# First stage of a long-convolution kernel: v pieces in output tiles, ten x buffers, one load for w1 and window, zeros multiplied at the start

## The chip, the cores and the metric

The kernel runs on one core of one Trainium2 chip. The metric is device microseconds of one execution, as the median of several; lower is better. In the views below PE is the matmul engine (TensorE) and PEld its weight loads, DVE is VectorE, ACT is ScalarE, POOL is GpSimd, and SP is SyncE, which does nothing here but issue DMAs. All engines run their own instructions strictly in program order and wait for each other by semaphores.

## What is computed

A causal convolution of length 12480 over 128 channels, done with FFTs, and then two feed-forward layers on the result:

```python
h_mlp = np.maximum(pos_emb @ w1, 0.0) @ w2          # filter, S x 128, hidden size 64
h_filt = h_mlp * np.exp(-0.01 * np.arange(S))[:, None]
u = x * v
Uf = np.fft.rfft(u, n=2 * S, axis=1)
Hf = np.fft.rfft(h_filt, n=2 * S, axis=0)
y = np.fft.irfft(Uf * Hf[None], n=2 * S, axis=1)[:, :S]
a = (x * y).reshape(S, 128)
h = np.maximum(a @ moe_w_in, 0.0);  a = (h * h) @ moe_w_out       # hidden size 2048
h = a @ moe2_w_in;  out = np.where(h > 0, h, np.exp(np.minimum(h, 0)) - 1) @ moe2_w_out
```

All inputs are float32, apart from the four feed-forward weights, which the kernel gets as 64-bit words and decodes.

## The kernel before

The FFT of length 181 x 127 is cut in two factors. `phase1` (the first stage, about the first 110 us of the span) does the factor of 181 by matmuls with a table `t1`, first for the filter and then for u. `phase2` does the factor of 127, multiplies the spectra and writes the product to DRAM; `phase3`, about four fifths of the span, does the inverse factor of 181 and the two feed-forward layers. The change touches `phase1` alone.

Inside `phase1` the work runs in four parts, and the code is written in the order in which each engine gets it:

- Eight filter steps (`zstep(s)`, "z steps" below): PE multiplies the piece `post[:, s]` of the position table (partly loaded by `load_pos`) by `w1`, which lies twice on the diagonal of a 128 x 128 block of zeros; 8 matmuls of 128 columns, 16 passes in the trace, L237. DVE takes the result out of PSUM with relu and the window (2 instructions, L241) into a buffer `fb`; then POOL adds and DVE subtracts its two halves (L246) into `fold`, which lies in `xu[2]` (the trace's m).
- Sixteen filter transform steps: `s1(i, ...)` with columns of `fold`, 8 matmuls of 182 columns, 16 passes, L263; ACT takes each result out into `xr` (L132 is the helper `copy`).
- The input pieces: x and v come in sixteen pairs. `load_xv(j)` issues four DMAs on SP (x piece and v piece, each as 98 rows and 1 row, 396 KB together). `ufold(j)` is three DVE instructions: v = x * v (L254), sum of its halves into x (L255), difference into x (L129). Before, x pieces have seven buffers (NX, tag xc) and v pieces three (NV, tag vc). Pieces 0 to 6 are loaded and folded beside the filter steps; after them piece j + 7 is loaded and folded behind the two transform steps that read piece j.
- Thirty-two u transform steps ("x steps"): `s1(i, ...)` on piece i // 2, again 16 passes of L263. Each result is taken out in four copies into the output tiles `xu[0]`, `xu[1]`, `xu[2]` (m in the trace) and `xt`. For i below 18 all four are ACT's (L132); from i = 18 on the first two are DVE's (L270) and ACT does the other two.

PSUM holds four result tiles for all of these steps (three rotate in pool `pss`; every fourth step uses `ps4`, which is closed near the end, at the 46th result, for a tile of the next stage). `prologue(i)` puts the first instructions of phase 2 between the x steps: loads of w2, g and six tables tb at i = 15, matmuls on the filter at i = 24 and i = 29.

So three queues matter around the change: SP, where the load of a piece waits for the buffer that it overwrites (x: for PE's reading of the piece seven before, v: for DVE's fold of the piece three before) and everything behind it waits too; DVE, where the copies of x steps 18 to 31 stand behind the last fold; and PE, which can run at most as many steps ahead as PSUM has tiles.

Of the kernel before, what the change touches and what calls it, by code (L numbers as in the profile page):

```python
# [10 lines left out]

F32 = mybir.dt.float32
F32R = mybir.dt.float32r
# [2 lines left out]
ALU = mybir.AluOpType  # L16
# [4 lines left out]
S = 12480  # L21
D = 128
E = 64
# [6 lines left out]
K1 = N1 // 2 + 1  # L30
NP = (K1 + 1) // 2
R = 99
# [9 lines left out]
WDEC = 11  # L42
OFF = 3
LAG1 = 2
NX = 7
NV = 3
NS1 = 46


def _angle(num, den):  # L50
# [18 lines left out]
def tables():  # L69
    n1 = np.arange(R)  # L70
    k1 = np.arange(K1)
    k2 = np.arange(N2)
    pe, po = np.arange(CEN + 1), np.arange(1, CEN + 1)
    t = {}
    th = _angle(n1[:, None] * k1[None, :], N1)
    t["t1"] = np.stack([np.cos(th), -np.sin(th), -np.cos(th)], axis=2).reshape(R, 3 * K1)
    tf = np.zeros((2 * NP, N2, N2))
    k = k1[:, None, None] + N1 * k2[None, None, :]
    tf[:K1, :CEN + 1] = np.cos(_angle(pe[None, :, None] * k, L))
    tf[:K1, 0] = 0.5  # L80
    tf[:K1, CEN + 1:] = np.sin(_angle(po[None, :, None] * k, L))
    t["tf"] = np.zeros((NP, 128, 2 * N2))
    t["tf"][:, :N2] = tf.reshape(NP, 2, N2, N2).swapaxes(1, 2).reshape(NP, N2, 2 * N2)
    th = _angle(k2[:, None] * pe[None, :], N2)
    g = np.zeros((128, 128))
    g[:N2, 0] = 1.0
    g[:N2, 1:N2:2] = np.cos(th)[:, 1:]
    g[:N2, 2:N2:2] = np.sin(th)[:, 1:]
    t["g"] = g
    order = [s * p for right, left, _ in _tiles() for s, ps in ((1, right), (-1, left)) for p in ps]  # L90
    c = np.where(k1 == 0, 1.0, 2.0)[:, None, None] / L
    th = _angle(k1[:, None, None] * (np.array(order)[None, :, None] + N2 * n1[None, None, :]), L)
    t["t3"] = np.stack([c * np.cos(th), -c * np.sin(th)], axis=2).reshape(K1, N2 * 2 * R)
    th = _angle((k[2 * PD:, 0, :, None, None] *
                 (np.array(order)[:SIZES[0], None] + N2 * n1[None, :R - 1])[None, None]), L).reshape(KD, N2, -1)
    t["t4"] = np.zeros((128, 2 * th[:, 0].size))
    t["t4"][:N2] = (2.0 / L * np.stack([np.cos(th), -np.sin(th)], axis=1)).transpose(2, 0, 1, 3).reshape(N2, -1)
    pos = _taps().astype(np.float32)
    ok = (pos >= 0) & (pos < S)
    win = np.where(ok, np.exp(np.float32(-0.01) * np.where(ok, pos, np.float32(0.0))), 0.0)  # L100
    t["win"] = win.transpose(2, 0, 1).reshape(R, 8, 2, 4, 2).transpose(0, 1, 2, 4, 3).reshape(R, 128)
    return {k: np.ascontiguousarray(a, dtype=np.float32) for k, a in t.items()}


# [14 lines left out]
class Build:  # L119
# [14 lines left out]
    def setup(self):  # L134
        nc = self.nc
        const = self.const = self.pool("const")
        self.dram = self.pool("dram", 1, DRAM)
        self.ident = const.tile([128, 128], F32, name="ident")
        make_identity(nc, self.ident)
        self.zero = const.tile([128, 2], F32, name="zero")  # L140
        nc.vector.memset(self.zero, 0.0)
        self.ebias = const.tile([128, 2], F32, name="ebias")
        nc.vector.memset(self.ebias[:, 0:1], 1151.0)
        nc.vector.memset(self.ebias[:, 1:2], 255.0 * 8388608.0)
        self.t1 = const.tile([R, K1, 3], F32, name="t1")
        self.Z = self.dram.tile([K1, 128, 2 * D], F32, name="Zd")
        self.wp = self.pool("wp")
        self.tiles = _tiles()
        self.st = {}
# [28 lines left out]
    def phase1(self):  # L178
        nc, a = self.nc, self.a
        with ExitStack() as ctx1:  # L180
# [7 lines left out]
            def stile(a, b):  # L188
                ns[0] += 1
                if ns[0] % 4 == 0 and ns[0] < NS1:  # L190
                    return ps4.tile([128, a, b], F32, tag="s", name="s")
                if ns[0] == NS1:
                    ctxs.close()
                    self.psb.append(self.ctx.enter_context(
                        self.tc.tile_pool(name="psb0", bufs=1, space=PSUM, side="right")))
                return pss.tile([128, a, b], F32, tag="s", name="s")
# [3 lines left out]
            self.xt = self.mid.tile([128, KTAIL * 2 * D], F32, name="xt")  # L200
            self.p2 = self.pool("p2")
            xvp = self.right.enter_context(self.tc.tile_pool(name="xv", bufs=1, side="right"))
            fbp = self.right.enter_context(self.tc.tile_pool(name="fb", bufs=2, side="right"))
            win, w1 = self.xt[:R, :128].rearrange("p (s c h n) -> p s c h n", s=8, c=2, h=2), self.xt[:, 128:256]
            post = self.xr[:, :64 * R].rearrange("p (s w) -> p s w", s=8)
            fold = self.xu[2][:R, :2 * C1 * E].rearrange("p (o n e) -> p o n e", o=2, e=E)

# [4 lines left out]

            def load_xv(j):
                for i, (d, nm, n) in enumerate(((xs, "xc", NX), (vs, "vc", NV))):
                    t = d[j] = xvp.tile([R, 8, 2, C1], F32, tag=nm, name=nm, bufs=n)
                    t = t.rearrange("p d h n -> p (d h n)")
                    for b, e in ((0, R - 1), (R - 1, R)):
                        nc.sync.dma_start(out=t[b:e], in_=a["xv"][j, i, b:e])

            nc.vector.memset(w1, 0.0)  # L220
            load_pos(0, 1)
            for p in range(2):
                nc.sync.dma_start(out=w1[E * p:E * p + E, E * p:E * p + E], in_=a["w1"])
            nc.sync.dma_start(out=self.xt[:R, :128], in_=a["win"])
            for b, e in ((1, 2), (2, 4), (4, 8)):
                load_pos(b, e)
            nc.sync.dma_start(out=self.t1.rearrange("p k a -> p (k a)"), in_=a["t1"])
            for j in range(NV):
                load_xv(j)

            def zstep(s):
                ps = stile(2, 512)
                z = ps[:R].rearrange("p c (h n e) -> p c h n e", h=2, e=E)
                for c in range(2):
                    for q in range(4):
                        i = 4 * c + q
                        nc.tensor.matmul(ps[:R, c, 128 * q:128 * q + 128], lhsT=post[:, s, i * R:i * R + R], rhs=w1,  # L237
                                         start=(q == 0), stop=(q == 3))
                f = fbp.tile([R, 2, 2, 4, E], F32, tag="f", name="fb")
                for c in range(2):  # L240
                    nc.vector.scalar_tensor_tensor(  # L241
                        out=f[:, c], in0=z[:, c], scalar=0.0,
                        in1=win[:, s, c].unsqueeze(3).to_broadcast([R, 2, 4, E]), op0=ALU.max, op1=ALU.mult)
                f = f.rearrange("p c h n e -> p c h (n e)")
                for o, (eng, op) in enumerate(((nc.gpsimd, ALU.add), (nc.vector, ALU.subtract))):
                    eng.tensor_tensor(out=fold[:, o, 8 * s:8 * s + 8].rearrange("p (c n) e -> p c (n e)", c=2),  # L246
                                      in0=f[:, :, 0], in1=f[:, :, 1], op=op)

            for s in range(8):
                zstep(s)  # L250
# [7 lines left out]
            def s1(i, fb, dst, w):  # L258
                ps = stile(2, 512)
                pv = ps[:, :, :4 * K1].rearrange("p b (c e) -> p b c e", e=2)  # L260
                for j in range(4):
                    for q, (b, e) in enumerate(((0, C1), (C1, N2))):
                        nc.tensor.matmul(pv[b:e, j // 2, :, j % 2], lhsT=fb[j][q], rhs=self.t1[:, :, q:q + 2],  # L263
                                         start=(j % 2 == 0), stop=(j % 2 == 1))
                b = 0
                for o, n in dst:
                    o = o.rearrange("p (c d) -> p c d", d=w)[:N2, :, 4 * i:4 * i + 4]
                    o, z = o.rearrange("p c (b e) -> p c b e", e=2), pv[:N2, :, b:b + n].rearrange("p b c e -> p c b e")
                    if n == 32 and i >= 2 * (16 - NX):
                        nc.vector.tensor_copy(o, z)  # L270
                    else:
                        self.copy(o, z)
                    b += n

            for j in range(NX):
                ufold(j)
                if j + NV < NX:
                    load_xv(j + NV)
                for i in range(2 * j, 2 * j + 2):
                    s1(i, [(fold[:, 0, :, 4 * i + c], fold[:, 1, 1:, 4 * i + c]) for c in range(4)],  # L280
                       [(self.xr, 2 * K1)], E)
            for i in range(2 * NX, E // 4):
                s1(i, [(fold[:, 0, :, 4 * i + c], fold[:, 1, 1:, 4 * i + c]) for c in range(4)], [(self.xr, 2 * K1)], E)
            dst = [(t, n) for t, n in zip(self.xu + [self.xt], (32, 32, 64, 2 * KTAIL))]
            self.raw = {}
# [557 lines left out]
```

## Time and profile before

| | us |
|---|---|
| median of 3 runs | 1429.74 |
| lowest and highest run | 1426.77, 1432.49 |
| the profiled execution | 1427.98 |
| its span, first to last instruction | 1426.2 |

| engine | busy us | share of the span |
|---|---|---|
| PE | 1372.2 | 96% |
| DVE | 1199.8 | 84% |
| ACT | 1109.0 | 78% |
| POOL | 617.6 | 43% |

The shares are averages over all three phases, and phase 3 with its matmuls rules them. A change of the first stage is read from windows and timelines of the first 110 us alone. The profiled execution lies 1.76 us under the median, inside the spread of the runs.

### The profile page before, as it was taken

Reading aid. Unit: us, or ns where it says so; the run is one execution under the profiler, and the core shown is the slowest. Engines: PE = TensorE matmul, PEld = TensorE weight load, DVE = VectorE, ACT = ScalarE, POOL = GpSimd, SP = SyncE. Lnnn points to the kernel's source line nnn. Section 1 sums busy time; section 2 is a strip of 40 time slices with the busy share of each in tenths; the row PEclk is TensorE's granted clock in tenths of the full one; section 3 lists DMA queues with packets and bytes.
Section 4 is the critical chain, followed back from the end, with each engine's and each line's share of the span. In section 5 each row is a group of like instructions: output and inputs, shape, how many; then the busy total and the mean of one; then the engine's idle time right before and its main releaser. Section 6 shows DMA issues by size and latency. Waiting matters only on the chain.

```text
span 1426.2 us, 19129 instructions
## 1 busy us (share of the span) xinstructions
PE 1372.2 (96%) x7228; PEld 1155.6 (81%) x7228; DVE 1199.8 (84%) x1295; ACT 1109.0 (78%) x1391; POOL 617.6 (43%) x343
## 2 busy tenths in 40 slices
PE   7959998999999999999999999999999999999997
PEld 6946665788888888888888888888888888888875
DVE  7547888688888988898888988889888898889887
ACT  1726676588888888888888888888888888888886
POOL 4005978354443434444444444444444344444431
PEclk9979999999999999999999999999999999999999
DMA  7635675401001110111101111011100111000000
GB/s 223 176 90 163 194 212 185 126 33 40 16 25 41 40 40 1 41 40 41 41 0 41 41 40 37 4 41 41 40 17 24 41 41 40 1 29 8 8 8 12
DMA packets 43291, 81.45 MB, mean 57 GB/s; under 512 B 4099, under 2 KB 32881, under 8 KB 43199
## 3 DMA queue, kind: packets, MB, share of 16 engines
q1 hardware_dynamic: 43199, 80.23, 18.6%
q8 instruction: 57, 0.93, 0.3%
q14 instruction: 35, 0.29, 0.1%
HBM read 61.85 MB, written 18.32 MB: 56 GB/s over the span
## 4 chain that ended last, share of the span: by engine, by line
PE 85%; DVE 4%; POOL 3%; DMA 3%; ACT 2%; issue 2%; SPq 1%; POOLq 0%; DVEq 0%; ACTq 0%
PE y L157 12%; PE h L156 12%; PE h L158 12%; PE y L158 12%; PE y L156 12%; PE h L157 12%; PE h L572 4%; PE s L263 3%; DMA vc<-in_xv_dram 2%; PE u L447 1%; PE v L470 1%; POOL pt L462 1%; PE h L327 1%; POOL pt L463 1%; POOL m L129 1%
## 5 line engine op out<-in xcount | busy, mean ns | idle before, releaser
L129 POOL TENSOR_TENSOR lo<-g,hi 128x980 fp32r<-128x980 f32 (+4 forms) x206 | 482.8, 2344 | 659.0 <-DVE tn L762 625.5
L797 ACT ACTIVATE tn<-h 128x980 f32<-128x980 f32 (+4 forms) x208 | 202.9, 976 | 177.7 <-PE h L158 165.6
L762 DVE SCALAR_TENSOR_TENSOR tn<-ex,tn 128x980 f32<-128x980 f32 (+4 forms) x208 | 241.1, 1159 | 118.4 <-ACT ex L798 116.2
L157 PE MATMUL y<-lo,m 128*128 128x490 f32 (+4 forms) x832 | 317.9, 382 | 6.2 <-POOL lo L129 3.2
L156 PE MATMUL y<-hi,m 128*128 128x490 f32 (+4 forms) x832 | 319.5, 384 | 4.0 <-ACT hi L132 1.7
L156 PE MATMUL h<-xh,m 128*128 128x490 f32 (+4 forms) x832 | 317.3, 381 | 1.8 <-DVE g L772 0.8
L158 PE MATMUL y<-hi,m 128*128 128x490 f32 (+4 forms) x832 | 317.3, 381 | 0.0
L158 PE MATMUL h<-xh,m 128*128 128x490 f32 (+4 forms) x832 | 316.9, 381 | 0.0
L157 PE MATMUL h<-xl,m 128*128 128x490 f32 (+4 forms) x832 | 315.9, 380 | 0.2 <-DVE xl L129 0.2
L129 DVE TENSOR_TENSOR lo<-ex,hi 128x980 fp32r<-128x980 f32 (+5 forms) x208 | 257.3, 1237 | 1.1 <-ACT hi L132 1.0
L772 DVE SCALAR_TENSOR_TENSOR g<-h,r 128x980 f32<-128x980 f32 (+4 forms) x208 | 239.6, 1152 | 12.0 <-ACT r L768 11.8
L789 DVE SCALAR_TENSOR_TENSOR ex<-tn,h 128x980 f32<-128x980 f32 (+4 forms) x208 | 238.3, 1146 | 0.6
L132 ACT ACTIVATE hi<-ex 128x980 fp32r<-128x980 f32 (+4 forms) x208 | 211.9, 1019 | 2.0 <-DVE ex L789 1.9
L779 ACT ACTIVATE hi<-r 128x980 fp32r<-128x980 f32 (+4 forms) x208 | 211.9, 1019 | 0.9
L768 ACT ACTIVATE r<-h 128x980 f32<-128x980 f32 (+4 forms) x208 | 204.0, 981 | 7.6 <-PE h L158 7.6
L798 ACT ACTIVATE ex<-h 128x980 f32<-128x980 f32 (+4 forms) x208 | 201.1, 967 | 0.0
L157 PEld LDWEIGHTS y<-lo,m 128*128 128x128 f32 x832 | 156.7, 188 | 36.5 <-POOL lo L129 5.6
L156 PEld LDWEIGHTS y<-hi,m 128*128 128x128 f32 x832 | 157.0, 189 | 34.5 <-ACT ys L132 4.6
L156 PEld LDWEIGHTS h<-xh,m 128*128 128x128 f32 x832 | 156.8, 188 | 29.9 <-DVE g L772 2.2
L157 PEld LDWEIGHTS h<-xl,m 128*128 128x128 f32 x832 | 156.9, 189 | 27.7 <-DVE xl L129 0.4
L158 PEld LDWEIGHTS y<-hi,m 128*128 128x128 f32 x832 | 156.9, 189 | 26.7
L158 PEld LDWEIGHTS h<-xh,m 128*128 128x128 f32 x832 | 156.7, 188 | 26.8
(81 smaller groups left out, 1161.3 us busy)
## 6 DMA issues: line engine op xcount, KB each, us to landing
z<-Zd SPq DMA_DIRECT2D x24, 546.0 KB
Zd<-z SPq DMA_DIRECT2D x45, 256.0 KB
t<-in_t_dram SPq DMA_DIRECT2D x24, 351.9 KB
xc<-in_xv_dram SPq DMA_DIRECT2D x16, 392.0 KB
vc<-in_xv_dram SPq DMA_DIRECT2D x16, 392.0 KB
tb<-in_tf_dram SPq DMA_DIRECT2D x46, 127.0 KB
raw<-in_moe_w_in_dram SPq DMA_DIRECT2D x8, 512.0 KB
raw<-in_moe_w_out_dram SPq DMA_DIRECT2D x8, 512.0 KB
```

Source lines behind the costliest of these rows:

```text
L129: return eng.tensor_tensor(out=out, in0=a, in1=b, op=ALU.subtract)
L132: self.nc.scalar.activation(out=out, in_=in_, func=AF.Copy)
L156: nc.tensor.matmul(out, lhsT=lhi, rhs=rhi, start=start, stop=False)
L157: nc.tensor.matmul(out, lhsT=lhi, rhs=rlo, start=False, stop=False)
L158: nc.tensor.matmul(out, lhsT=llo, rhs=rhi, start=False, stop=stop)
L762: after = nc.vector.scalar_tensor_tensor(out=pa["em"], in0=pa["ex"], scalar=1.0, in1=pa["tn"], op0=ALU.add, op1=ALU.mult)
L768: nc.scalar.activation(out=f["r"], in_=f["h"], func=AF.Relu)
L772: nc.vector.scalar_tensor_tensor(out=f["g"], in0=f["h"], scalar=0.0, in1=f["r"], op0=ALU.max, op1=ALU.mult)
L779: nc.scalar.activation(out=f["hi"], in_=f["r"], func=AF.Square)
L789: nc.vector.scalar_tensor_tensor(out=pa["g"], in0=pa["em"], scalar=0.0, in1=pa["h"], op0=ALU.min, op1=ALU.max)
L797: nc.scalar.activation(out=e["tn"], in_=e["h"], func=AF.Tanh, scale=0.5)
L798: nc.scalar.activation(out=e["ex"], in_=e["h"], func=AF.Exp)
```

## The change

- `load_xv`: the v pieces 0 to 7 no longer have buffers of their own; each is a quarter of `xu[0]` (pieces 0 to 3) or `xu[1]` (4 to 7), the tiles into which the x steps write later. x pieces have ten buffers instead of seven, v pieces from 8 on have two. Pieces 0 to 7 are issued at once, 8 and 9 behind them; piece j + 10 is loaded and folded behind the x steps of piece j.
- `fb`, the first-layer result of a z step, lies in two parts of `xt` instead of a pool of its own.
- `w1` comes as a ready block, with the window, in one load of 128 x 256 words; before, DVE cleared the block and two loads filled it, and a third one brought the window.
- In the last z step POOL adds only the first half of the columns; DVE adds the second half after its subtraction.
- PE multiplies a tile of zeros six times (NWARM, 12 passes of 128 columns) before the z steps; the result tile is one of the rotating PSUM tiles, so the count at which `ps4` closes rises by one (NS1). The identity matrix that POOL built, and which nothing used, is gone.
- DVE takes the first two copies of an x step from i = 20 on (ND), not from 18 on; ACT does four more copies.

```diff
-NX = 7
-NV = 3
-NS1 = 46
+NX = 10
+NV = 2
+ND = 20
+NWARM = 6
+NS1 = 47
...
             def load_xv(j):
                 for i, (d, nm, n) in enumerate(((xs, "xc", NX), (vs, "vc", NV))):
-                    t = d[j] = xvp.tile([R, 8, 2, C1], F32, tag=nm, name=nm, bufs=n)
-                    t = t.rearrange("p d h n -> p (d h n)")
+                    if i and j < 8:
+                        t = self.xu[j // 4][:R, 1024 * (j % 4):1024 * (j % 4) + 1024]
+                    else:
+                        t = xvp.tile([R, 1024], F32, tag=nm, name=nm, bufs=n)
+                    d[j] = t.rearrange("p (d h n) -> p d h n", d=8, h=2)
...
-            nc.vector.memset(w1, 0.0)
             load_pos(0, 1)
-            for p in range(2):
-                nc.sync.dma_start(out=w1[E * p:E * p + E, E * p:E * p + E], in_=a["w1"])
-            nc.sync.dma_start(out=self.xt[:R, :128], in_=a["win"])
+            nc.sync.dma_start(out=self.xt[:, :256], in_=a["wz"])
+            ps = stile(2, 512)
+            for i in range(NWARM):
+                nc.tensor.matmul(ps[:, 0, :128], lhsT=self.zero, rhs=self.zero, start=True, stop=True)
...
-            for j in range(NV):
+            for j in range(8):
                 load_xv(j)
...
-                f = fbp.tile([R, 2, 2, 4, E], F32, tag="f", name="fb")
+                f = fb[s % 2]
...
+                if s == 7:
+                    parts = [(nc.gpsimd, 0, slice(0, 1)), (nc.vector, 1, slice(0, 2)), (nc.vector, 0, slice(1, 2))]
...
-                    if n == 32 and i >= 2 * (16 - NX):
+                    if n == 32 and i >= ND:
                         nc.vector.tensor_copy(o, z)
...
             for j in range(NX):
                 ufold(j)
-                if j + NV < NX:
-                    load_xv(j + NV)
+                if 8 <= j + 8 < NX:
+                    load_xv(j + 8)
```

SP's queue where phase 2's first loads are issued, before: w2, g and tb stand ahead of the last two pairs of pieces.

```order
L218 DMA vc<-in_xv_dram 98x1024
L218 DMA vc<-in_xv_dram 1x1024
L341 DMA w_715<-in_w_dram 64x128 x2
L342 DMA g<-in_g_dram 128x128
L300 DMA tb<-in_tf_dram 128x254 x6
L218 DMA xc<-in_xv_dram 98x1024
L218 DMA xc<-in_xv_dram 1x1024
```

The same place of SP's queue in the changed kernel:

```order
L221 DMA xc<-in_xv_dram 98x1024
L221 DMA xc<-in_xv_dram 1x1024
L221 DMA vc<-in_xv_dram 98x1024
L221 DMA vc<-in_xv_dram 1x1024
L344 DMA w_714<-in_w_dram 64x128 x2
L345 DMA g<-in_g_dram 128x128
L303 DMA tb<-in_tf_dram 128x254 x6
```

The last pair of pieces has moved from behind the nine loads of w2, g and tb to ahead of them.

DVE's instructions at the end of the z steps and the start of the folds, before (m_89 is `fold`):

```order
L241 SCALAR_TENSOR_TENSOR fb<-s,xt 99x512 x2
L246 TENSOR_TENSOR m_89<-fb 99x512
L254 TENSOR_TENSOR vc<-xc,vc 99x1024
L255 TENSOR_TENSOR xc<-vc 99x8x64
L129 TENSOR_TENSOR xc<-vc 99x8x64
```

The same place on DVE in the changed kernel (m_84 is `fold`, m_82 is `xu[0]`):

```order
L244 SCALAR_TENSOR_TENSOR xt<-s,xt 99x512 x2
L252 TENSOR_TENSOR m_84<-xt 99x512
L252 TENSOR_TENSOR m_84<-xt 99x256
L260 TENSOR_TENSOR m_82<-xc,m_82 99x1024
L261 TENSOR_TENSOR xc<-m_82 99x8x64
```

The half-width addition has come in ahead of the first fold, and the v piece of that fold lies in `xu[0]`.

## Rows read from the trace of the kernel before

**Rows 1.** PE's waits, first 95 us: total, times, longest

```profile
PE s L263 <- ACT xt L132: 16.7, 1, 16.7
PE s L237 <- DMA xc<-in_xv_dram: 5.6, 1, 5.6
PE s L263 <- POOL m L246: 4.3, 1, 4.3
```

**Rows 2.** Windows, PE: stretch, length, busy (instructions), granted clock, DMA share, GB/s

```profile
48.00:75.40 27.40, 27.40 (x356) 1.00 0.75 213
75.40:92.10 16.70, 0.01 (x1) 0.59 0.55 146
92.10:98.70 6.60, 6.59 (x44) 0.50 0.00 0
```

**Rows 3.** Timeline, end of the stall: start, length, instruction, idle before and releaser

```profile
88.31 1.23 DVE L254 TENSOR_TENSOR vc<-xc,vc 99x1024 f32<-99x1024 f32 x1 [0.44 <-DMA vc<-in_xv_dram]
90.85 1.67 DVE L270 COPY m<-s 127x128 f32<-127x128 f32 x8
91.43 0.38 ACT L132 ACTIVATE m<-s 127x256 f32<-127x256 f32 x1 [19.95 <-DVE m L270]
```

**Rows 4.** Timeline of SP's DMA issues, with the start of each

```profile
1.19 1.21 SPq L223 DMA_DIRECT2D xt<-in_w_dram  x2
...
36.07 0.62 SPq L218 DMA_DIRECT2D vc<-in_xv_dram  x2
50.76 0.62 SPq L218 DMA_DIRECT2D xc<-in_xv_dram  x2
...
73.93 3.93 SPq L300 DMA_DIRECT2D tb<-in_tf_dram  x6
77.96 0.66 SPq L218 DMA_DIRECT2D xc<-in_xv_dram  x2
```

**Rows 5.** Timeline of DVE: folds that waited for their v piece

```profile
56.18 1.23 DVE L254 TENSOR_TENSOR vc<-xc,vc 99x1024 f32<-99x1024 f32 x1 [10.96 <-DMA vc<-in_xv_dram]
...
60.38 1.22 DVE L254 TENSOR_TENSOR vc<-xc,vc 99x1024 f32<-99x1024 f32 x1 [1.57 <-DMA vc<-in_xv_dram]
...
73.85 1.23 DVE L254 TENSOR_TENSOR vc<-xc,vc 99x1024 f32<-99x1024 f32 x1 [1.04 <-DMA w<-in_w_dram]
```

**Rows 6.** Window over the first pieces, columns as in rows 2, all engines

```profile
11.90:23.70 11.80, 10.07 (x93) 9.85 (x91) 11.60 (x20) 1.28 (x1) 10.62 (x7) 1.00 0.89 244
```

**Rows 7.** Windows of PE, filter steps, columns as in rows 2

```profile
5.60:9.20 3.60, 3.60 (x17) 1.00 1.03 407
10.10:21.90 11.80, 11.80 (x109) 1.00 0.93 273
...
27.20:30.50 3.30, 3.30 (x24) 0.50 0.21 45
```

**Rows 8.** Timeline of DVE, first z steps

```profile
9.33 1.29 DVE L241 SCALAR_TENSOR_TENSOR fb<-s,xt 99x512 f32<-99x512 f32 x2 [8.25 <-PE s L237]
10.66 0.69 DVE L246 TENSOR_TENSOR m<-fb 99x512 f32<-99x512 f32 x1
11.52 0.69 DVE L241 SCALAR_TENSOR_TENSOR fb<-s,xt 99x512 f32<-99x512 f32 x1 [0.18 <-PE s L237]
```

**Rows 9.** Timeline of POOL and DVE, last z step and first folds

```profile
24.44 1.77 POOL L246 TENSOR_TENSOR m<-fb 99x512 f32<-99x512 f32 x1 [0.15 <-DVE fb L241]
...
25.01 2.29 DVE L254 TENSOR_TENSOR vc<-xc,vc 99x1024 f32<-99x1024 f32 x1
...
28.54 1.22 DVE L254 TENSOR_TENSOR vc<-xc,vc 99x1024 f32<-99x1024 f32 x1
...
31.00 1.23 DVE L254 TENSOR_TENSOR vc<-xc,vc 99x1024 f32<-99x1024 f32 x1
```

**Rows 10.** Timeline of one late x step: DVE's copies, ACT's last copy

```profile
103.07 0.49 DVE L270 COPY m<-s 127x128 f32<-127x128 f32 x2 [0.74 <-PE s L263]
...
103.93 0.34 ACT L132 ACTIVATE xt<-s 127x216 f32<-127x216 f32 x1
```

More of the change, by code (lines that the diff above doesn't have):

```diff
@@ L9 @@
 from concourse.bass_utils import run_bass_kernel_spmd
-from concourse.masks import make_identity
 F32 = mybir.dt.float32
@@ L100, in tables @@
     win = np.where(ok, np.exp(np.float32(-0.01) * np.where(ok, pos, np.float32(0.0))), 0.0)
-    t["win"] = win.transpose(2, 0, 1).reshape(R, 8, 2, 4, 2).transpose(0, 1, 2, 4, 3).reshape(R, 128)
+    win = win.transpose(2, 0, 1).reshape(R, 8, 2, 4, 2).transpose(0, 1, 2, 4, 3).reshape(R, 128)
+    t["wz"] = np.concatenate([win, np.zeros((128 - R, 128))])
     return {k: np.ascontiguousarray(a, dtype=np.float32) for k, a in t.items()}
@@ L137, in setup @@
         self.dram = self.pool("dram", 1, DRAM)
-        self.ident = const.tile([128, 128], F32, name="ident")
-        make_identity(nc, self.ident)
-        self.zero = const.tile([128, 2], F32, name="zero")
+        self.zero = const.tile([128, 128], F32, name="zero")
         nc.vector.memset(self.zero, 0.0)
@@ L202, in phase1 @@
             xvp = self.right.enter_context(self.tc.tile_pool(name="xv", bufs=1, side="right"))
-            fbp = self.right.enter_context(self.tc.tile_pool(name="fb", bufs=2, side="right"))
             win, w1 = self.xt[:R, :128].rearrange("p (s c h n) -> p s c h n", s=8, c=2, h=2), self.xt[:, 128:256]
+            fb = [self.xt[:R, o:o + 1024].rearrange("p (c h n e) -> p c h n e", c=2, h=2, e=E) for o in (256, 1280)]
             post = self.xr[:, :64 * R].rearrange("p (s w) -> p s w", s=8)
@@ L244, in zstep @@
                 f = f.rearrange("p c h n e -> p c h (n e)")
-                for o, (eng, op) in enumerate(((nc.gpsimd, ALU.add), (nc.vector, ALU.subtract))):
-                    eng.tensor_tensor(out=fold[:, o, 8 * s:8 * s + 8].rearrange("p (c n) e -> p c (n e)", c=2),
-                                      in0=f[:, :, 0], in1=f[:, :, 1], op=op)
+                parts = [(nc.gpsimd, 0, slice(0, 2)), (nc.vector, 1, slice(0, 2))]
+                if s == 7:
+                    parts = [(nc.gpsimd, 0, slice(0, 1)), (nc.vector, 1, slice(0, 2)), (nc.vector, 0, slice(1, 2))]
+                for eng, o, c in parts:
+                    eng.tensor_tensor(out=fold[:, o, 8 * s:8 * s + 8].rearrange("p (c n) e -> p c (n e)", c=2)[:, c],
+                                      in0=f[:, c, 0], in1=f[:, c, 1], op=(ALU.add, ALU.subtract)[o])
             for s in range(8):
@@ L276, in phase1 @@
                 ufold(j)
-                if j + NV < NX:
-                    load_xv(j + NV)
[L279 to L282, printed above, removed]
+                if 8 <= j + 8 < NX:
+                    load_xv(j + 8)
+            for i in range(E // 4):
                 s1(i, [(fold[:, 0, :, 4 * i + c], fold[:, 1, 1:, 4 * i + c]) for c in range(4)], [(self.xr, 2 * K1)], E)
@@ L823 @@
     arrays = {
-        "xt": np.ascontiguousarray(x.reshape(S, D)[perm].T), "xv": xv, "post": post, "w1": w1, "w2": w2,
+        "xt": np.ascontiguousarray(x.reshape(S, D)[perm].T), "xv": xv, "post": post, "w2": w2,
     }
@@ L829 @@
     arrays.update(tables())
+    w = np.zeros((128, 128), np.float32)
+    w[:E, :E] = w[E:, E:] = w1
+    arrays["wz"] = np.concatenate([arrays["wz"], w], axis=1)
     arrays = {k: np.ascontiguousarray(t) for k, t in arrays.items()}
```

## The prediction

> **What bounds the kernel now.** I read the first stage alone, since the later ones see the change only as an earlier start. First PE's waits [rows 1]: three waits in 95 us, and one of them, 16.7 us, is larger than the others together. The windows [rows 2] show what lies around it: 27.40 us of gapless work on the x steps, then 16.70 us with nothing, then 6.60 us at a granted clock of 0.50, which is the lower of its two levels (1.2 GHz), after PE had idled. The name behind the wait is ACT's copy, but that is only the last link. The timeline of the end of the stall [rows 3] reads backwards: ACT had sat idle for 19.95 us until DVE's copy at 90.85; this copy stands behind DVE's last fold, which began at 88.31 when its v piece had landed. The queue of loads [rows 4] tells why that piece was late: after 36.07 no piece is issued until 50.76, when PE has read the first x piece and so freed a buffer, and the last two pairs stand behind the table loads of 73.93 (3.93 us of issuing) and start at 77.96. So the chain is: few buffers, late loads, late folds, copies behind the folds on DVE, PSUM full, PE idle. Ahead of that the stage has a second bound: PE begins at 5.6 us and DVE takes the first result at 9.33 [rows 1, 8].
>
> **The change part by part.** I call c the time at which the x steps begin; before it is about 48.0 [rows 2]. One x step costs PE 27.40 / 22 = 1.245 us (22 of the 32 steps lie in that window, 352 of the 512 passes).
>
> *Stall.* With ten x buffers, and v pieces 0 to 7 in tiles that nobody needs yet, twenty pieces can be loaded without waiting for PE. They move at 244 GB/s [rows 6]; a piece has 99 x 4096 bytes, so 1.66 us. Starting at about 11, the sixteenth (v 7) lands at 11 + 16 x 1.66 = 37.6 and the twentieth at 44.2, under work that takes that long anyway. DVE folds a pair every 31.00 - 28.54 = 2.46 us [rows 9], so folds 0 to 9 end about 10 x 2.46 after the z steps; with the front's 2.0 us (below) the first fold ends at 26.6, fold 7 at 43.8 and fold 9 at 48.7. This hides the new wait of the change: ACT's copies into xu[0] and xu[1] must wait for folds 3 and 7, which still read v there. The first copy is due at c + 1.25 = 47.3 with c = 46.0, so 3.5 us of cover; if it were gone, ACT, and through PSUM PE, would stand behind DVE.
>
> Only six pairs are left. The first is issued when x step 1 is through, and DVE gets it 56.18 - 48.0 = c + 8.2 at the pace of the same event before (issue at 50.76, c + 2.8; fold at 56.18) [rows 4, 5]. Five intervals later the last fold begins. Their length: five such intervals before took 73.85 - 56.18 = 17.67, so 3.53 each, the longest one 4.20 [rows 5]. The last fold starts at c + 25.8, ends at c + 28.3; DVE's copies for step 20 and ACT's behind them take 104.27 - 103.07 = 1.2 us [rows 10], so step 20's PSUM tile is free at c + 29.5. PE wants that tile again three steps on, for step 23, at c + 23 x 1.245 = c + 28.6. A stall of 0.9 us remains. Bounds: 0 (if the pieces come at the 2 x 1.66 of the streaming rate, the last fold ends a microsecond earlier) and 4.2 (if each interval is the longest, 4.20: 5 x 0.67 = 3.3 more). So 16.7 goes and 0.9 comes: **-15.8**. The two steps 18 and 19 that go back to ACT cost nothing: ACT does four copies in each earlier step within PE's 1.245. The phase 2 loads now stand behind the last pair on SP: v 15 goes out when fold 13 is over, at c + 8.2 + 3 x 3.53 + 2.46 = c + 21.3, and the tables take 3.93 us of issuing behind it; their first reader is the filter matmul after step 24, at 25 x 1.245 + 0.9 = c + 32, so their landing is covered.
>
> *Clock.* 6.60 us at half speed after the stall [rows 2] are 3.3 us lost. Without an idle stretch this goes: **-3.3**. PE also idles 4.3 us between z steps and filter transform [rows 1], and 3.30 us behind it are at 0.50 [rows 7], a loss of 1.65. Both ends of that gap move together, so it stays; whether the clock falls there may differ from run to run: 0, bounds -1.65 and +1.65.
>
> *Front.* z step 0 waits for w1 and the first piece of the table. One load goes out where the first half of w1 went at 1.19, and the second half, 0.6 us behind it, is gone [rows 4]; the position pieces move up by twice that. I take 0.6 earlier; bounds 0 (the piece of the table was last) and 1.2. Before, step 0 ran slowly: 17 passes in 3.60 us, 0.212 each, against 109 in 11.80, 0.108 each [rows 7]. The page's granted clock says 1.00 there, but the spacing is that of the lower level. Sixteen passes are 3.4 us at one pace and 1.7 at the other. The twelve passes over zeros take 2.5 us from about 1.2 on, while PE has nothing to do, so they cost nothing themselves. Before, the fast pace came 4.5 us after PE's first work (5.6 to 10.1). If work on zeros counts as work, it would now come near 5.7, soon after z step 0 begins at 5.0. I take 1.0 saved; bounds 0 and 1.7. Behind step 0 DVE sets the pace, 11.52 - 9.33 less the wait of 0.18, so about 2 us per step [rows 8], and those 0.18 go as well.
>
> *Last fold.* POOL's addition ends at 26.2 and PE starts there. Halved, it would end near 25.4, and DVE's added half (half of 0.69 [rows 8]) after its subtraction likewise: 0.8 saved, if the two engines run side by side. The row speaks against it: the fold at 25.01 took 2.29 where others take 1.22 [rows 9], 1.06 more, and POOL's addition overlapped it for 1.2. Then the three pieces come one after another: 0.69, half of (1.77 - 0.65) = 0.56 and 0.35 end at 26.0. I take 0.2, the value of the nearer row; bounds 0.1 and 0.8. The Trainium skill (SBUF — State Buffer, section "SBUF: two separate sides") says that DVE with two SBUF inputs and GpSimd take a shared pair of ports as a lock for the whole instruction, so the other fully blocks; the trace agrees with 2.29 against 1.22. By that rule this edit gives the 0.2, without it the forecast would be 0.6 lower.
>
> Front together: 0.6 + 1.0 + 0.18 + 0.2 = **-2.0** (0.3 to 3.9). c becomes 46.0.
>
> *Nothing:* memsets and the identity (under 0.5 us on POOL and DVE, before any data), buffers for fb in xt (two as before, and the copies into xt come 20 us later), PSUM count (the zeros use one tile that nobody reads).
>
> *Sum:* -15.8 - 3.3 - 2.0 = -21.1. The profiled execution would go from 1427.98 to 1406.9, the median of 1429.74, 1.76 above it, to **1408.6**.
>
> **The rivals.**
> *Late last folds.* v 12 to 15 now wait for the fold two before them, since there are two v buffers instead of three. If every interval is as long as the longest, 4.20 [rows 5], the stall is 4.2 instead of 0.9: 1411.9. For it: the lock-step is new. Against: a fold and a fresh load, 2.46 + 5.4 (50.76 to 56.18), serve two buffers, 3.9 per pair, hardly more than 3.53.
> *The z steps get in each other's way.* Results, window and w1 now lie in one tile. If PE's next step waited until DVE had written, each of eight steps would cost 1.7 + 1.3 instead of 2, some 8.5 in all: 1417; with late folds beside it 1420 or more, at the edge of no change. Against: the instruction order of the changed kernel puts no more between the matmuls than before, and regions of one tile (the pieces of the position table in xr) are already used one by one.
> *Slower: the output tiles become a gate.* ACT cannot take out x step 0 until fold 7 is done. It decides nothing up to 3.5 us of delay. To eat the whole 21.1, fold 7 would have to end at 47.3 + 21.1 = 68.4, so v 7 to land at 65.9, (65.9 - 11) / 16 = 3.4 us per piece; 7.1 us slower (1437) takes 3.9 us per piece, 104 GB/s. Against: 244 GB/s over six pieces in a row [rows 6]; nothing else loads in that time.
>
> **How the numbers follow.** Forecast 1408.6 with 0.68, own range 1404 to 1411; late folds (1411.9) 0.20; better than that range (front and last fold at their good ends, no low clock before the filter transform) 0.04; z steps in each other's way 0.05, of which 0.03 at the edge of no change; slower 0.03. What measurement can tell from no change is about 0.5%, 7.1 us. Faster: 0.68 + 0.20 + 0.04 + 0.02 = 0.94; same 0.03; slower 0.03. The range: best sum 16.7 + 3.3 + 3.9 + 1.65 = 25.6, so 1404.2; worst sum 16.7 - 4.2 + 3.3 + 0.3 - 1.65 = 14.4, so 1415.3. The runs before lie up to 3 us from their median, so I take 1402 to 1416.
>
> **What would show it.** PE's waits in the first 90 us should have no entry over 5 us; x steps should fill a window of 41 to 44 us that begins near 46, at a granted clock of 1.00 throughout; phase 2 should begin about 21 us earlier. DVE's last fold should end near 74, two to three steps before PE needs it. The first z result should reach DVE near 7.7. I am wrong if DVE waits for v pieces 10 to 15 for longer than 4.2 per pair, if ACT waits for DVE at x step 0, or if z step 0 still takes 3.4 us.

## The result

| | before | predicted | after |
|---|---|---|---|
| median, us | 1428.72 (4 runs) | 1408.6 | 1410.20 (4 runs, 1407.08 to 1411.17) |
| the profiled execution | 1427.98 | 1406.9 | 1411.12 |
| its span | 1426.2 | | 1409.0 |

The ratio is 0.9864, 95% interval 0.9836 to 0.9891. The change takes 18.5 us by the medians and 16.9 by the two profiled executions, where 21.1 were predicted; the time lies in the range of 1402 to 1416.

PE's waits in the first 95 us of the changed kernel (total, times, longest) stand against [rows 1]:

```profile
PE s L269 <- DVE m L252: 3.7, 1, 3.7
PE s L269 <- ACT xt L134: 2.6, 1, 2.6
...
PE s L240 <- DMA xr<-in_post_dram: 0.9, 1, 0.9
```

The wait of 16.7 has become 2.6. The one before the filter transform steps, 4.3, is 3.7. And there is a wait that the kernel before did not have: 0.9 us for the position table, in the middle of the z steps.

The windows of the x steps (stretch, length, PE busy with instructions, granted clock, DMA share, GB/s) answer to [rows 2]:

```profile
45.80:74.30 28.50, 28.50 (x370) 1.00 0.71 196
74.30:76.90 2.60, 0.04 (x3) 0.87 0.43 126
76.90:83.00 6.10, 6.10 (x37) 0.50 0.00 0
83.10:93.60 10.50, 10.50 (x133) 1.00 0.01 2
```

The x steps begin at 45.8 instead of 48.0 and their last stretch ends at 93.6 instead of 110.4. In between, a stall of 2.6 us still lies where the long one was, and behind it stand 6.1 us at half clock, almost what stood there before (6.60).

The end of that stall, in the timeline of DVE, ACT and PE (start, length, instruction, idle before and releaser), has the same links as [rows 3]:

```profile
73.10 1.22 DVE L260 TENSOR_TENSOR vc<-xc,vc 99x1024 f32<-99x1024 f32 x1 [1.35 <-DMA vc<-in_xv_dram]
...
75.64 1.27 DVE L276 COPY m<-s 127x128 f32<-127x128 f32 x6
...
76.21 0.38 ACT L134 ACTIVATE m<-s 127x256 f32<-127x256 f32 x1 [4.58 <-DVE m L276]
...
76.89 0.87 PE L269 MATMUL s<-t,xc 99*64 99x182 f32 x4 [2.56 <-ACT xt L134]
```

The last fold starts at 73.10 instead of 88.31; DVE's copies of step 20 and after stand behind it, ACT behind them, PE behind ACT. So the chain is the one that was read before; only its length changed.

Added up by the two profiles: x steps 2.2 earlier, stall 16.7 - 2.56 = 14.1 less, half clock 3.3 - 3.05 = 0.25 less, together 16.6 of the 16.86 us.

The first z steps in the timeline of PE and DVE (compare [rows 8]):

```profile
4.39 7.85 PE L240 MATMUL s<-xt,xr 128*99 128x128 f32 x64 [0.42 <-DMA xt<-in_wz_dram]
...
6.45 1.29 DVE L244 SCALAR_TENSOR_TENSOR xt<-s,xt 99x512 f32<-99x512 f32 x2 [5.44 <-PE s L240]
...
13.16 7.20 PE L240 MATMUL s<-xt,xr 128*99 128x128 f32 x64 [0.91 <-DMA xr<-in_post_dram]
...
15.22 1.29 DVE L244 SCALAR_TENSOR_TENSOR xt<-s,xt 99x512 f32<-99x512 f32 x2 [0.68 <-PE s L240]
```

DVE has its first result at 6.45 instead of 9.33, 2.9 us earlier. Four steps later PE stands and waits for the last load of the position table (steps 4 to 7, one transfer of 1.6 MB), and DVE waits with it: a first part of the gain is given back there.

### The profile page after: what moved, and what is told of

Its sections match the earlier page's. It is cut to its first block, busy times and chain, and to the rows that moved or that the text cites. A ratio compares the mean times of both kernels' runs of the same rounds, so it can differ in the third digit from the quotient of the medians.

```text
span 1409.0 us, 19136 instructions
## 1 busy us (share of the span) xinstructions
PE 1373.3 (97%) x7240; PEld 1156.8 (82%) x7240; DVE 1198.3 (85%) x1291; ACT 1109.2 (79%) x1395; POOL 616.2 (44%) x341
## 4 chain that ended last, share of the span: by engine, by line
PE 85%; DVE 4%; DMA 4%; POOL 3%; ACT 2%; issue 1%; SPq 0%; POOLq 0%; DVEq 0%; ACTq 0%
PE y L157 12%; PE h L156 12%; PE h L158 12%; PE y L158 12%; PE y L156 12%; PE h L157 12%; PE h L575 4%; PE s L269 3%; DMA xc<-in_xv_dram 1%; DMA vc<-in_xv_dram 1%; PE u L450 1%; PE v L473 1%; POOL pt L465 1%; PE h L330 1%; POOL pt L466 1%
```

## The experiments

What the theories A and B say in each of them is told in its expectation. e1 to e4 ran on one chip, e5 to e8 on another, e9 and e10 on the first one again; the kernel before had medians of 1427.89, 1427.70 and 1428.37 beside them.

**The copies start later: e1_copies_from_24.**

```diff
-ND = 20
+ND = 24
```

> The changed kernel with DVE's first copies starting at x step 24 instead of 20; ACT does all four copies of steps 20 to 23 too. Theory A (the rest of the stall, 2.56 us in the changed kernel, is DVE's copies of step 20 standing behind its last fold, which ends at 75.7, while ACT has room: 0.97 of work per step of 1.245): the wait of PE on ACT near 74 falls under 0.5 us, the granted clock stays at 1.00 through the x steps (6.2 us at 0.50 in the changed kernel, 3.1 lost), phase 2 starts about 5.5 us earlier, time near 1404.5. Rival B (ACT itself becomes the bound once it keeps all copies, with the filter's copy rr of 0.6 us behind step 24): the steps 20 to 24 take more than 1.3 us each and the gain stays under 2 us. Rival C (the half clock has nothing to do with the idle stretch): the stall goes but some 6 us at 0.50 remain, gain 2.5 us.

Measured: 1407.00 (4 runs, 1406.93 to 1408.53), ratio 0.9855 (0.982 to 0.989), where theory A expected 1404.5. PE's timeline:

```profile
15.01 7.20 PE L240 MATMUL s<-xt,xr 128*99 128x128 f32 x64 [1.98 <-DMA xr<-in_post_dram]
...
25.88 21.92 PE L269 MATMUL s<-t,m 99*64 99x182 f32 x256 [3.68 <-DVE m L252]
...
47.61 31.04 PE L269 MATMUL s<-t,xc 99*64 99x182 f32 x400
```

With the copies of steps 20 to 23 on ACT, the 400 passes up to phase 2's filter matmuls run in one piece: no stall, no half clock. So what ended last after the change was indeed DVE's copies queued behind late folds. The profiled execution is 4.2 us under that of after, though its x steps begin 1.8 later; stall and half clock had cost 2.56 + 3.05 = 5.6, and 5.6 - 1.8 = 3.8. So the mechanism of theory A is what the rows show, and its time was missed by the late start. The late start has its cause in the first row: the table's last load was waited for until 15.01.

**The front alone: e2_front_only.** Buffers, order of loads and copies as before; one load for w1, zeros, divided last fold and `fb` in `xt` as in the change.

```diff
-NX = 10
-NV = 2
-ND = 20
+NX = 7
+NV = 3
+ND = 18
...
-                    if i and j < 8:
-                        t = self.xu[j // 4][:R, 1024 * (j % 4):1024 * (j % 4) + 1024]
-                    else:
-                        t = xvp.tile([R, 1024], F32, tag=nm, name=nm, bufs=n)
+                    t = xvp.tile([R, 1024], F32, tag=nm, name=nm, bufs=n)
...
-            for j in range(8):
+            for j in range(NV):
```

> The front of the change alone: one load for window and w1, zeros multiplied, split last fold, results in xt; but seven x buffers, three v buffers and copies from step 18 as before. Theory A (the stall before hangs on the time at which PE frees the first x piece, so it moves with the front): filter transform starts near 24.0 instead of 26.3, the stall is 16 to 17 us again, and the whole gains about 2.2 us on before. Rival B (the late pieces are bound by the loads as such, from the start of the program): the stall grows by what the front gave, gain 0.

Measured: 1427.55 (10 runs), ratio 0.9997 (0.9978 to 1.0017), that is anything from 3.1 us of gain to 2.4 of loss. The gain of about 2 us that theory A expected is not seen, but the times do not rule it out. PE's timeline, of an execution that took 1431.42:

```profile
24.70 22.97 PE L266 MATMUL s<-t,m 99*64 99x182 f32 x256 [3.67 <-DVE m L249]
...
47.41 27.39 PE L266 MATMUL s<-t,xc 99*64 99x182 f32 x352
...
92.72 6.78 PE L266 MATMUL s<-t,xc 99*64 99x182 f32 x48 [17.93 <-ACT xt L134]
```

The filter transform starts 1.56 us earlier than before (26.26) but takes longer, since its first 5.8 us had a granted clock of 0.52; the x steps begin 0.6 earlier; and the stall is 17.93 instead of 16.7, because the last two folds (85.38 and 88.41) stand where they stood before (85.25 and 88.31). In this execution, whatever the front wins is waited out. The loads of the last two pairs still stand behind the table loads on SP, and went out at 79.22 instead of 77.96.

**The buffers alone: e3_loads_only.** The kernel before with ten x buffers, v pieces in output tiles, `fb` in `xt`, the order of the loads, and ND of the change; its own front.

```diff
-NX = 7
-NV = 3
+NX = 10
+NV = 2
+ND = 20
...
+                    if i and j < 8:
+                        t = self.xu[j // 4][:R, 1024 * (j % 4):1024 * (j % 4) + 1024]
...
-            for j in range(NV):
+            for j in range(8):
...
-                    if n == 32 and i >= 2 * (16 - NX):
+                    if n == 32 and i >= ND:
```

> The buffers of the change alone (ten x buffers, v pieces 0 to 7 in output tiles, two v buffers, copies from step 20, results in xt), with the window, w1 in two loads, no zeros and the unsplit last fold as before. Theory A (parts add): filter transform starts near 26.2, x steps near 48, a stall of 2 to 4 us is left, gain on before 14 to 16 us if the clock falls again after the stall, 17 to 19 if not. Rival B (the front gives nothing in the end because the table's last piece lands at 13 in both kernels): the gain is that of the whole change, 17 to 19, with the same low clock.

Measured: 1409.24 (4 runs, 1408.22 to 1413.40), ratio 0.9872 (0.984 to 0.9905): 18.65 us of gain, as much as the whole change. PE's timeline:

```profile
4.55 16.02 PE L241 MATMUL s<-xt,xr 128*99 128x128 f32 x128 [4.55 <-DMA xt<-in_w_dram]
24.96 21.98 PE L267 MATMUL s<-t,m 99*64 99x182 f32 x256 [4.39 <-POOL m L250]
...
46.77 28.58 PE L267 MATMUL s<-t,xc 99*64 99x182 f32 x368
76.84 2.69 PE L267 MATMUL s<-t,xc 99*64 99x182 f32 x32 [1.48 <-ACT xt L133]
```

And its windows of PE (columns as above):

```profile
75.30:76.80 1.50, 0.05 (x2) 1.00 0.86 245
76.80:79.50 2.70, 2.66 (x33) 1.00 0.00 0
```

The old front, too, can bring the filter transform to 24.96 in a run: z step 0 starts at 4.55 here, with the same loads with which it started at 5.59 before, and no step waited for the table. The stall is 1.48 and the clock stays at 1.00 behind it. Between the profiled executions of before and e3 lie 1427.98 - 1408.22 = 19.8 us: 15.2 of stall, 3.3 of clock and 1.3 by which the x steps begin earlier. So the buffers and what goes with them carry the gain; which part of this bundle is needed for it was not taken apart.

**No zeros: e4_no_zeros.**

```diff
-NWARM = 6
-NS1 = 47
+NWARM = 0
+NS1 = 46
...
-            ps = stile(2, 512)
-            for i in range(NWARM):
-                nc.tensor.matmul(ps[:, 0, :128], lhsT=self.zero, rhs=self.zero, start=True, stop=True)
```

> The changed kernel without the six matmuls over zeros. In the changed kernel the first result reaches DVE at 6.45, but z step 4 waits for the last piece of the position table until 13.16, and DVE with it until 15.22. Theory A (the table's load sets the front, not PE's clock): the first z steps run at the slow spacing of 0.21 us per pass and the first result reaches DVE near 8, but step 4 is still ready near 15.2 and the filter transform starts within 0.8 us of 24.03. Rival B (the zeros carry the front's gain): the filter transform starts 1.5 to 2 us later, near 25.8.

Measured: 1415.94 in its one run. DVE's timeline has the first result at 8.20 instead of 6.45:

```profile
8.20 1.29 DVE L241 SCALAR_TENSOR_TENSOR xt<-s,xt 99x512 f32<-99x512 f32 x2 [7.19 <-PE s L237]
```

But 6.45 is the best of eight. In e1, whose front is that of after, DVE has:

```profile
7.58 1.29 DVE L244 SCALAR_TENSOR_TENSOR xt<-s,xt 99x512 f32<-99x512 f32 x2 [6.56 <-PE s L240]
```

From the start of z step 0 to its result there are 3.74 or 3.75 us in the four kernels without zeros (before, e3, e4, e10) and 2.06 (after) to 3.21 (e1) in the eight profiles with them. So the zeros bring the fast pace somewhere within z step 0, and save 0.5 to 1.7 us there. What that is worth at the end this run does not tell: z step 4 waited for the table until 14.59, and the filter transform began at 25.47, 1.44 later than in after, of which the table's later landing (14.59 against 13.16) is 1.43. The x steps began at 47.18, and the stall of 3.16 was followed by 9 us at half clock.

**The table step by step: e5_table_by_step_24,** with the copies of e1.

```diff
-ND = 20
+ND = 24
...
-            for b, e in ((1, 2), (2, 4), (4, 8)):
+            for b, e in ((1, 2), (2, 3), (3, 4), (4, 5), (5, 6), (6, 7), (7, 8)):
```

> The changed kernel with two edits: the position table comes in eight loads, one per z step, instead of four (1, 1, 2 and 4 steps), and DVE's copies start at x step 24. In the kernels with the new front PE waited 0.6 to 2.0 us for the table's last load (four steps' worth), which landed at 13.0 to 14.9. Theory A (the front is set by when the whole last load has landed, not by the clock or by DVE): step 4 no longer waits, z steps follow each other at DVE's 1.93 us, the filter transform starts at 22.8 to 23.3 instead of 24.0 to 25.9; with the stall gone as in the run with copies from 24, time 1404 to 1406. Rival B (the DMA engines are full until 12 us and each step's load lands late as well): waits of the same sum spread over steps 4 to 7, filter transform at 24 to 26, time as with copies from 24 alone, near 1407. Rival C (the pieces, now issued later, reach the folds late, and the first copies into xu[1] wait for fold 7): a wait of ACT on DVE near x step 0 of 1 us or more.

Measured: 1406.27 (5 runs, 1404.13 to 1408.13), ratio 0.9847 (0.9825 to 0.987), the lowest median of all, though not clear of e1's 1407.00. PE's timeline:

```profile
4.46 14.39 PE L240 MATMUL s<-xt,xr 128*99 128x128 f32 x128 [0.48 <-DMA xt<-in_wz_dram]
...
23.16 22.92 PE L269 MATMUL s<-t,m 99*64 99x182 f32 x256 [4.32 <-DVE m L252]
...
45.90 31.04 PE L269 MATMUL s<-t,xc 99*64 99x182 f32 x400
```

All 128 passes of the z steps run without a wait, DVE takes a result every 1.93 us from 6.66 to 20.14, and the filter transform starts at 23.16, the earliest of all. ACT did not wait for DVE at x step 0, as rival C would have it: its first copy there, at 47.36, was released by PE. The early start is not kept whole, as the window there shows:

```profile
23.10:28.50 5.40, 5.34 (x36) 0.50 0.91 243
```

Half of 5.4 us is lost behind the wait of 4.32. Beside e1, the x steps begin 1.7 earlier and the profiled execution ends 0.66 earlier; the medians, from two chips, differ by 0.7.

**The changed kernel again: e6_changed_again,** beside e5 on the same chip.

> The changed kernel once more, beside the others on the same chip. Theory A (its last stall is a little over or under 2.5 us and the clock falls in some executions): median 1409 to 1411, a wait of PE on ACT of 1.5 to 3.5 us after x step 22, and 0 to 9 us at a granted clock of 0.50 behind it. Rival (the stall of the first profile was a chance): no wait over 1 us.

Measured: 1411.27 (6 runs, 1406.23 to 1413.82), ratio 0.9874 (0.9848 to 0.99). e5's median is 5.0 us lower; the two ratios' intervals overlap by 0.0022, and two of the six runs (1406.23 and 1407.68) lie among e5's. PE's timeline again has a stall near the end:

```profile
77.78 5.12 PE L269 MATMUL s<-t,xc 99*64 99x182 f32 x32 [2.19 <-ACT xt L134]
```

with 6.6 us at half clock behind it (window of PE):

```profile
77.70:84.40 6.70, 6.62 (x39) 0.50 0.00 0
```

Together 2.19 + 3.3 = 5.5 us, about the 5.0.

**Three v buffers: e7_three_v_nine_x.**

```diff
-NX = 10
-NV = 2
+NX = 9
+NV = 3
```

> The changed kernel with nine x buffers and three v buffers instead of ten and two (the same memory). Theory A (two v buffers tie each late v load to the fold two before it, which spreads the last folds from 3.5 to 3.85 us apart): SP's waits on DVE shrink from 7.5 us to under 3, the last folds are 3.4 to 3.6 apart; seven pairs instead of six are late, so the last fold starts at c + 8.1 + 6 x 3.5 = c + 29, later than the c + 27.3 of the changed kernel, and the stall is 4 us. Rival B (the DMA engines' rate sets the spacing): the spacing stays at 3.8, the last fold starts at c + 31 and the stall is over 5.5 us.

Measured: 1415.17 in its one run. SP's waits between 44 and 85 us (total, times, longest):

```profile
SPq L221 <- PE s L269: 12.6, 4, 11.0
SPq L221 <- DMA xc<-in_xv_dram: 5.5, 5, 1.5
SPq L221 <- DMA vc<-in_xv_dram: 4.1, 5, 1.2
```

After has another row in the same view of its 44 to 75 us:

```profile
SPq L221 <- PE s L269: 7.7, 5, 4.6
SPq L221 <- DVE xc L131: 7.5, 4, 2.8
```

With the third buffer SP no longer waits for DVE's folds when it loads the pieces, and the folds stand 3.37 us apart instead of 3.85. That would be theory A's price for two buffers, but other runs with two have 3.38 (e9), 3.39 (e10), 3.45 (e5) and 3.46 (e1), and two kernels with three have 3.53 (before) and 3.85 (e2). The runs of one setting differ as much as the settings. What spaces the folds is not settled by this. The time is worse than that of after because one x piece fewer is loaded ahead (the last fold starts at c + 29.4, the stall is 4.58) and the z steps waited 2.2 us for the table.

**The last fold undivided: e8_unsplit_last_fold.**

```diff
-                if s == 7:
-                    parts = [(nc.gpsimd, 0, slice(0, 1)), (nc.vector, 1, slice(0, 2)), (nc.vector, 0, slice(1, 2))]
```

> The changed kernel with POOL adding all columns of the last z step, as before. Theory A (POOL and DVE take turns on these instructions): the filter transform starts 1.9 us after the last relu ends, against 1.74 in the changed kernel, so the split is worth 0.1 to 0.2 us, and the first fold's product on DVE again takes 2.2 to 2.3 us. Rival B (they run side by side): 0.6 us or more later than in the changed kernel, counted from the last relu.

Measured: 1415.33 in its one run, with a wait of 2.86 us for the table, so the time says nothing of the edit. The timeline of DVE, POOL and PE does:

```profile
24.18 1.28 DVE L244 SCALAR_TENSOR_TENSOR xt<-s,xt 99x512 f32<-99x512 f32 x2
...
25.50 0.69 DVE L250 TENSOR_TENSOR m<-xt 99x512 f32<-99x512 f32 x1
25.54 1.77 POOL L250 TENSOR_TENSOR m<-xt 99x512 f32<-99x512 f32 x1 [0.16 <-DVE xt L244]
26.10 2.29 DVE L258 TENSOR_TENSOR m<-xc,m 99x1024 f32<-99x1024 f32 x1
...
27.36 0.91 PE L267 MATMUL s<-t,m 99*64 99x182 f32 x4 [3.83 <-POOL m L250]
```

The same place of after:

```profile
20.44 2.45 POOL L252 TENSOR_TENSOR m<-xt 99x512 f32<-99x512 f32 x2 [0.15 <-DVE xt L244]
21.01 1.28 DVE L244 SCALAR_TENSOR_TENSOR xt<-s,xt 99x512 f32<-99x512 f32 x2
...
22.32 1.45 DVE L252 TENSOR_TENSOR m<-xt 99x512 f32<-99x512 f32 x2
...
23.70 1.21 DVE L260 TENSOR_TENSOR m<-xc,m 99x1024 f32<-99x1024 f32 x1
```

From the end of the last relu to the start of the filter transform there are 27.36 - 25.46 = 1.90 us undivided and 24.03 - 22.29 = 1.74 divided: the edit is worth 0.16, not 0.8. The other profiles agree: 1.90 in before and e3, which do not divide it either, and 1.69 to 1.75 in the eight others that do. And the first fold's product, beside POOL's full addition, takes 2.29 again, against 1.21 where POOL is through. The two engines take turns. The Trainium skill (SBUF — State Buffer, section "SBUF: two separate sides") calls the ports that GpSimd shares with a VectorE instruction of two SBUF inputs an exclusive lock for the whole instruction; by that rule 0.2 was forecast, and both rows agree with it.

**The pieces held back: e9_pieces_held.** The table `t1` comes in five loads instead of one, which holds v piece 0 and x piece 1 back until the last load of the position table has landed (SP issues them at 14.37 and 15.03, in after at 4.33 and 6.45); x piece 0 still runs beside it.

```diff
-            nc.sync.dma_start(out=self.t1.rearrange("p k a -> p (k a)"), in_=a["t1"])
+            for b, e in ((0, 18), (18, 36), (36, 54), (54, 72), (72, K1)):
+                nc.sync.dma_start(out=self.t1[:, b:e].rearrange("p k a -> p (k a)"), in_=a["t1"][:, 3 * b:3 * e])
```

> The changed kernel with the t1 table in five loads instead of one. Eight loads can be open at once, so the extra ones hold back the first pieces: v 0 now waits for the table's last load instead of being issued at 4.3 beside it; only x 0 still runs beside it. Theory A (the last load of the position table lands late, at 13.0 to 16.3 in seven kernels with the new front, because the first three pieces share the DMA engines with it): it lands at 10.5 to 12, PE does not wait for it at z step 4, filter transform at 22.8 to 23.5. Rival B (a load of four steps' table is late by itself): PE still waits 0.6 us or more at z step 4 and the filter transform starts after 24.

Measured: 1411.11 in its one run. PE's timeline:

```profile
14.49 7.20 PE L241 MATMUL s<-xt,xr 128*99 128x128 f32 x64 [1.51 <-DMA xr<-in_post_dram]
```

The load of four steps is as late as in the other runs, so contention with these two pieces is not why. The theory that expected an earlier landing falls; that `t1` or x piece 0 holds the load up was not tried. What the DMA engines did while the table came in, before and then after (stretch, length, granted clock, DMA share, GB/s), tells more:

```profile
6.00:10.00 4.00, 1.00 1.02 406
10.00:13.00 3.00, 1.00 1.01 362
```

```profile
6.00:10.00 4.00, 1.00 1.02 408
10.00:13.00 3.00, 1.00 0.98 331
```

The sixteen engines were full in both kernels, so a load that is issued earlier only waits longer in line. Nor had the whole table landed much earlier in e5: ACT, whose first copy goes where the table lies, waited for it until 12.9 before, 13.1 in after and 12.6 in e5. There the steps did not wait, since each needs only its own piece. What differs between runs of the new front is the slowest part of the load: of its sixteen landing marks in the trace the first comes at 11.1 to 11.9 us (12.0 before), the last at 13.0 to 16.2 (12.8 before). Why that part is late stays open.

**The best version without zeros: e10_by_step_no_zeros.** e5 with the edit of e4.

> The kernel with the table by step and copies from x step 24, without the matmuls over zeros. There the table no longer sets the front: the first result reached DVE at 6.66 and the filter transform began at 23.16. Theory A (then PE's slow pace in z step 0 counts): the first result reaches DVE near 8.2, as in the changed kernel without zeros, and the filter transform starts 1.0 to 1.8 us later, at 24.2 to 25.0. Rival B (the front absorbs it): 23.2 to 23.6.

Measured: 1406.69 in its one run. PE's timeline:

```profile
4.49 16.48 PE L237 MATMUL s<-xt,xr 128*99 128x128 f32 x128 [4.49 <-DMA xt<-in_wz_dram]
...
25.11 21.97 PE L266 MATMUL s<-t,m 99*64 99x182 f32 x256 [4.14 <-DVE m L249]
...
46.82 31.09 PE L266 MATMUL s<-t,xc 99*64 99x182 f32 x400
```

The pace shows in the window of PE over z step 0, first here and then in e5 (columns as above):

```profile
4.50:7.90 3.40, 3.40 (x16) 1.00 0.86 286
```

```profile
4.50:7.90 3.40, 3.40 (x30) 1.00 1.01 375
```

Sixteen passes against thirty in the same time, both at a granted clock that reads 1.00. Where nothing waits for the table, the zeros are worth 25.11 - 23.16 = 1.95 us at the start of the filter transform, about what z step 0's slow pace costs. That is the value of this pair of runs: e5's first result, at 6.66, was one of the early ones. Half of it is gone at the start of the x steps (46.82 against 45.90), because e5's filter transform lost 2.7 us to the clock (5.4 at 0.50) and this one 1.7 (3.0 at 0.69 and 2.9 at 0.73), and at the end 0.4 is left, less than runs of one kernel differ.

## Why the prediction came out as it did

**The stall, -15.8.** The mechanism held in every link: twenty pieces land without waiting for PE, fold 7 ends at 45.2 and so before ACT's first copy, six pairs are left, and the last fold decides. So did the formula, stall = start of the last fold - c - 24.9: the last fold began at c + 27.3, which gives 2.4, and 2.56 was measured. It holds for each profile with copies from step 20 on and more than seven x buffers: 0.9 by the formula and 1.00 measured in e8, 1.4 and 1.48 in e3, 1.7 and 1.79 in e9, 2.1 and 2.19 in e6, 3.1 and 3.16 in e4, 4.5 and 4.58 in e7. The input was off. It took the spacing of the folds from one run of the kernel before, 3.53, and after had (73.10 - 53.86) / 5 = 3.85. Over the runs with two v buffers the spacing goes from 3.38 to 3.88, by which the formula gives stalls of 0.2 to 2.7 us; stalls of 1.0 to 3.2 were measured with ten x buffers and copies from step 20 on. The bounds of 0 to 4.2 held, the value inside them was taken from too little. The other input scatters too: in e9 the spacing was only 3.38, but the first late fold began at c + 9.7 instead of c + 8.2, and the stall was 1.79. The rival of late last folds (1411.9) was thus half right: between it and the forecast lies the result. That its cause is the two v buffers, e7 did not show.

**The clock, -3.3.** This is the term that was mis-sized: in the profile of after it is -0.25. I let the half clock go with the stall, although the same sum left 0.9 us of stall and allowed up to 4.2; even the worst sum of the range keeps the whole 3.3. The runs show otherwise. Idle time of PE in the stall, and the work at half clock behind it: 1.0 us (e8) and 1.48 (e3) none; 1.79 (e9) 4.2 us at 0.59 on average; 2.19 (e6) 6.6; 2.56 (after) 6.1; 3.16 (e4) 9.0; 4.58 (e7) 4.4; and the 16.7 of before 6.6 [rows 2]. A stall of 2 us costs as much clock as one of 17. Behind a stall of 0.9 the clock might have held, as it did in e8; behind the one that came it did not. e1, e5 and e10 have no stall and get the 3.3 as well.

**The front, -2.0.** In the profile of after c is 2.2 earlier, which looks like a hit and is none. One load for w1 instead of two was counted at 0.6; in the profile of after z step 0 starts 1.2 earlier (4.39 against 5.59), but e3 starts it at 4.55 with the old loads, so no gain of that edit is shown. The zeros were counted at 1.0 and save 0.5 to 1.7 from run to run (see e4), the most of them in after. The divided fold is worth 0.16 where 0.2 stood. But the prediction took DVE's pace of 2 us for the only bound behind step 0. The position table's last load is a second one: it had landed by 12.9 before, early enough for the steps of that kernel, and with the new front, issued 1.3 us earlier, it is waited for until 13.2 to 16.3 in all eight kernels that load it in one piece. With it the filter transform starts anywhere between 24.0 and 27.4, while the old front has 26.26 (before) and 24.96 (e3). What the front is worth in the time no run shows: alone it gives a ratio of 0.9997 (e2, with the interval told there), and the buffers without it give as much as the whole change (e3). The sentence that failed is "the position pieces move up by twice that": their issue did, their landing did not. The DMA engines were full from 6 us on with either front (see e9); why the last part of the load comes up to 3 us later in some runs stays open.

**Half clock before the filter transform, 0 with bounds of 1.65 either way.** It did change from run to run, as written: 5.8 us at 0.52 in e2, 5.4 at 0.50 in e5, 5.9 at about 0.7 in e10.

**Nothing.** The edits that were costed at nothing cost nothing that shows: the x steps' passes keep their pace (31.04 us for 400 in e1 and e5), ACT's copies into `xu[0]` did not wait for fold 7, and the phase 2 loads behind the last pair were in time. The cover of 3.5 us over fold 7 was 45.8 + 1.25 - 45.2 = 1.9.

**The sum.** By the profiles: -14.1 - 0.25 - 2.2 = -16.6 against -21.1. The missing 4.5 us are 1.7 of stall and 3.05 of clock, less 0.2. Their source is one spacing of folds, 0.32 us each, five times over.

## What to carry to other kernels

A stall that is made six times shorter, as here from 16.7 to 2.56 us, may still cost its whole loss of clock; either count the clock loss for any stall that is left, or add the last bit of slack, as e1 did by taking the copies of four more steps off the queue behind the late work. Price a faster start by the landing time of every load that the faster steps will ask for, since an earlier issue is not an earlier landing; if its readers need it piece by piece, load it piece by piece, as e5 did. And where one input, here the spacing of loads, is multiplied by five, take it from several runs before you trust a difference of microseconds.

## What the runs showed of the hardware

- PE's granted clock fell to 0.50, the lower level, with stalls of 2.19 and 2.56 us (and for a part of the 4.2 us behind one of 1.79, 0.59 on average), not with 1.0 and 1.48, one profile each; the loss, 1.7 to 4.5 us, did not grow with the stall.
- Multiplying zeros brought PE to its fast pace early: with them, z step 0 gave its result 2.06 to 3.21 us after its start (eight profiles), without them 3.74 or 3.75 (four), while the granted clock reads 1.00 for all. So early in the span the spacing of passes tells the clock, not the column.
- A load of 1584 KB in one piece was waited for until 13.2 us in one run and 16.3 in another, in kernels that issued it alike, the DMA engines being full meanwhile; the same bytes in four loads of 396 KB made no step wait, and were no sooner complete (12.6).
